# Loading the key cache as four heads of 32 partitions: a change to a two-block cached-attention kernel

## The chip, the cores and the metric

The kernel runs on one core of a Trainium2 chip. The metric is the device time of one execution in microseconds (us). The kernel before has a median of 908.98 us over 3 runs (905.89 to 911.09).

A core has five instruction streams that run side by side and meet at semaphores: TensorE (PE, with its weight loads shown apart as PEld), VectorE (DVE), ScalarE (ACT), GpSimd (POOL) and SyncE (SP). Sixteen DMA engines move data between HBM and SBUF. In this kernel SP issues all loads and ACT issues the sixteen stores.

## The reference, cut to what matters

Two independent blocks, A and B, of the same shape, each with its own inputs:

```python
B, Sq, D = 16, 64, 640;  H, Sk, Dh = 32, 512, 128        # bf16
q = (x @ wq).reshape(B, Sq, H, Dh).transpose(0, 2, 1, 3)
scores = einsum("bhqd,bhkd->bhqk", q, k_cache) * Dh ** -0.5
p = softmax(scores, axis=-1)
o = einsum("bhqk,bhkd->bhqd", p, v_cache)
block = o.transpose(0, 2, 1, 3).reshape(B, Sq, H * Dh) @ wo
out = concatenate([block_A, block_B], axis=-1)            # 16 x 64 x 1280
```

The key and the value cache are 67 MB each per block, 268 MB in all. The sum over keys in the softmax and in p·v doesn't depend on the order of the keys, as long as p and v have the same one.

## The kernel before, in words

**Tiling.** Two batches make a pair, so that 2 x 64 queries fill 128 partitions. A *step* is one head for a pair. Two steps are a *macro* (index m), two macros (four heads) a *chunk* (index c); 16 heads for one pair are a *group* (four chunks); the eight pairs of one block and one half of its heads are a *pass*. There are 4 passes, 128 chunks, 256 macros, 512 steps. The output of a pair is added up in PSUM over the 16 heads of a group; the first half's result is kept in `outp`, the second half adds it and stores.

**Work of a step or chunk.** Each kind of work has a two- to four-letter name in the code:

- QP4 (PE, line 481): the queries of four heads, 20 matmuls; QE4 (ACT, 490) copies them out.
- KX (PE, 465): transposes one K buffer, 32 instructions of 64 columns; KE (DVE, 473) copies the result into one of three `ktp` slots.
- SM (PE, 497): scores of one step, two matmuls of 512 columns that run together, one per batch; MX (DVE, 506) takes the row maximum, EX (ACT, 512) the exponential with its row sum, RC2 (DVE, 518) the reciprocals, NM (POOL, 526) multiplies and permutes the keys into the order that V has.
- TR (PE, 535) transposes p, TE (ACT or DVE, 544 and 546) copies it out, PV4 (PE, 556) multiplies by V for a chunk, OE4 (ACT, 564) copies out.
- OP (PE, 572): output product, columns 0 to 511, for one macro. At the end of a group OX (PE, 582) does columns 512 to 639 for all 16 heads at once, and OVP/OXP (ACT, 590 and 595; first half) or OVF/OXF (DVE, 600 and 605; second half) take the result out, then ST stores.

**What sets the order.** Templates written out by hand (`PE_T`, `ACT_T`, `DVE_T`, `POOL_T` in `Cfg`, lines 31 to 39) give each kind an offset in macros or chunks and a nominal time in a chunk's period; `build_plan` repeats them for all chunks and sorts. Every engine runs its list in order. `build_plan` derives the dependences from named resources (buffers and PSUM banks) and turns them into semaphore waits. In the list of PE a chunk runs SM four times, KX, PV4, OP, TR, KX, TR, OP, then OX in the last chunk of a group, then QP4.

PSUM has eight banks: one for OP, one shared by QP4 and PV4 (`QOB`), four for scores (`SB` 0 to 3; TR uses 0 and 1, OX uses 2) and two for KX.

**Loads.** LDK (line 651) brings for macro m and one batch two heads, 64 partitions each, 8 keys (2 KB) per partition: 256 KB. Two of them make one of ten K buffers, and KX of macro m needs both. LDV (660) brings two heads for one batch: 256 KB, 1 KB runs; four make one of five V buffers. LDWQ (629) and LDWO (637) bring the weights of four heads in two parts each, into six slots.

SP issues the loads in one list. `pace_loads` (line 338) adds a wait to most of them: it steps through a planned timeline of PE and of the transfers (constants `PE_NS`, `RATE`, `QUEUE_NS`, `START_NS`) and ties each load to the PE operation after which it's to be issued, so that about `QUEUE_NS` of work is ahead of it. A load therefore starts when PE reaches a certain place in its own program.

Of the kernel before, what the change touches and what calls it, by code (L numbers as in the profile page):

```python
# [5 lines left out]
BF16 = mybir.dt.bfloat16  # L6
# [8 lines left out]
class Cfg:  # L15
    G = 4
    HH = 16
    NKU = 10
    NVB = 5
# [6 lines left out]
    NT = 4  # L26
# [4 lines left out]
    PE_T = (("SM", 0, 0, 0.0), ("SM", 0, 1, 0.21), ("SM", 1, 0, 0.43), ("SM", 1, 1, 0.64), ("KX", 2, 0, 0.96),  # L31
            ("PV4", -2, 0, 1.53), ("OP", -5, 0, 2.47), ("TR", -2, 0, 2.9), ("KX", 3, 0, 3.45), ("TR", -1, 0, 4.03),
            ("OP", -4, 0, 4.47), ("OX", -5, 0, 4.9), ("QP4", 2, 0, 4.92))
    ACT_T = (("EX", 0, 0, 1.13), ("EX", 0, 1, 1.79), ("OVP", -5, 0, 2.92), ("OE4", -2, 0, 2.95), ("EX", 1, 0, 3.52), ("EX", 1, 1, 4.18),
             ("TE", -1, 0, 4.84), ("OXP", -5, 0, 5.9), ("ST", -5, 0, 6.0), ("QE4", 2, 0, 6.27))
    DVE_T = (("MX", 0, 0, 0.44), ("MX", 0, 1, 1.06), ("KE", 2, 0, 1.68), ("RC2", 0, 0, 2.83), ("OVF", -5, 0, 2.92),
             ("MX", 1, 0, 2.97), ("MX", 1, 1, 3.59), ("TE", -2, 0, 4.21), ("KE", 3, 0, 4.83),
             ("OXF", -5, 0, 5.9), ("RC2", 1, 0, 5.98))
# [4 lines left out]
    QUEUE_NS = 800.0  # L43
    START_NS = 1030.0
    RATE = dict(LDK=384.0, LDV=344.0, LDWQ=344.0, LDWO=354.0, LDX=160.0)
    DMA_NS = dict(LDK=700.0, LDV=760.0, LDWQ=950.0, LDWO=950.0, LDX=700.0)
# [22 lines left out]
def build_plan(dims, cfg):  # L69
# [30 lines left out]
    def make_chunk(eng, kind, c, ts):  # L100
        ps_, bp, _, h0 = step_info(G * c)
        if kind == "QP4":
            return mk(eng, "QP4", c, [("xT", bp)] + [("wq", wslot(ps_, h0 // G), i) for i in range(2)], [("QOB",)], ts)
        if kind == "QE4":
            return mk(eng, "QE4", c, [], [("QOB",)] + [("qT", m % cfg.NQ) for m in (2 * c, 2 * c + 1)], ts)
        if kind == "PV4":
            return mk(eng, "PV4", c, [("pT", m % cfg.NT) for m in (2 * c, 2 * c + 1)] + [("v", c % cfg.NVB, i) for i in range(4)],
                      [("QOB",)], ts)
        return mk(eng, "OE4", c, [], [("QOB",)] + [("oT", m % cfg.NO) for m in (2 * c, 2 * c + 1)], ts)

    def make_macro(eng, kind, m, sub, ts):
# [4 lines left out]
        if kind == "KX":  # L116
            return mk(eng, "KX", m, [("kn", m % cfg.NKU, 0), ("kn", m % cfg.NKU, 1), ("ident",)], [("KTB",)], ts)
        if kind == "KE":
            return mk(eng, "KE", m, [], [("KTB",), ("ktp", m % cfg.NKT)], ts)
        if kind == "SM":  # L120
            return mk(eng, "SM", (m, sub), [("qT", m % cfg.NQ), ("ktp", m % cfg.NKT)], [("SB", g % cfg.NS)], ts)
# [13 lines left out]
        if kind == "OP":  # L135
            return mk(eng, "OP", m, [("oT", m % cfg.NO), ("wo", wslot(ps_, h0 // G), m % 2)], [("OUTB",)], ts)
        if h0 + 2 != SPB:
            return None
        if kind == "OX":
            return mk(eng, "OX", m, [("oT", i % cfg.NO) for i in range(m + 1 - MPG, m + 1)]  # L140
                      + [("wo", wslot(ps_, i), n) for i in range(HG) for n in range(2)], [("SB", 2)], ts)
# [35 lines left out]
    for ps_ in range(NPASS):  # L177
        for j in range(HG):
# [7 lines left out]
            for part in range(2):  # L186
                add(rq, at["QP4", c0, 0], at["QP4", c0, 0], 0, "LDWQ", (ps_, j, part),
                    [("wq", wslot(ps_, j), part)], (ps_, j, part), cfg.DMA_NS["LDWQ"])
                first = at["OP", 2 * c0 + part, 0]
                add(ro, first, first, 3, "LDWO", (ps_, j, part), [("wo", wslot(ps_, j), part)], (ps_, j, part),  # L190
                    cfg.DMA_NS["LDWO"])

# [7 lines left out]
    for c in range(NCHUNK):  # L200
        for j in range(2):
# [3 lines left out]
            for b in range(2):  # L205
                add(ready, first, first, 2, "LDK", (m, b), [("kn", m % cfg.NKU, b)], (m, b), cfg.DMA_NS["LDK"])
            ready = at["PV4", c - cfg.NVB, 0] if c >= cfg.NVB else NEG
            first = at["PV4", c, 0]
            for i in (2 * j, 2 * j + 1):
                add(ready, first, first, 2.5, "LDV", (c, i), [("v", c % cfg.NVB, i)], (c, i), cfg.DMA_NS["LDV"])  # L210
# [15 lines left out]
    def sem_key(op):  # L226
# [4 lines left out]
        if op.kind in ("LDWQ", "LDWO"):  # L231
            return ("d_" + op.kind[2:].lower(),) + op.writes[0][1:]
# [139 lines left out]
def schedule(progs, cfg):  # L372
    def nbytes(op):
        if op.kind == "LDX":
            return (op.aux[2] - op.aux[1]) * (5 << 15)
        return dict(LDK=1 << 18, LDV=1 << 18, LDWQ=5 << 16, LDWO=5 << 16)[op.kind]
# [6 lines left out]
def mha_kernel(nc, blocks, out, cfg=None):  # L383
# [32 lines left out]
    with contextlib.ExitStack() as es:  # L416
# [9 lines left out]
        kn_ring = sb("kn_ring", [128, NKU, 2, 8, DH], BF16)  # L426
# [327 lines left out]
```

## Time and profile before

| What | Value |
|---|---|
| Median of 3 runs | 908.98 us |
| Profiled execution: its own time | 908.61 us |
| Profiled execution: span, first to last instruction | 906.8 us |
| TensorE clock granted, mean | 0.992 |
| PE busy / DVE / ACT / POOL | 836.8 / 722.4 / 652.5 / 416.8 us |
| Loads issued by SP | 1,094 |
| Moved | 297.51 MB, mean 328 GB/s |
| Median from issue to landing, K and V loads | 5.3 to 5.4 us |

How to read it: busy times are unions of instruction intervals, so engines overlap. "Idle before" a group is the time its engine waited just ahead of it, with what ended the wait; "issue" there means that the profile shows nothing that it waited for. A wait counts for the total only if the engine is the one that sets the pace at that place. The trace also has every instruction's start and every DMA packet with its size and duration; counts over these records are named as such.

### The profile page before, as it was taken

The numbers are of one execution on the slowest core, as the hardware profiler recorded it, in microseconds if no ns is written. First come the engines' busy times: TensorE is split into PE (matmuls) and PEld (weight loads), VectorE is DVE, ScalarE is ACT, GpSimd is POOL, SyncE is SP. The second block draws the span as 40 slices with busy tenths as digits, with TensorE's granted clock in tenths as the row PEclk, the third lists the DMA queues.
The fourth block names the chain that finished last, engine by engine and source line by source line (L and its number), as shares of the span: only waits on it lengthen the run. The fifth ranks groups of instructions, "written<-read, shape, count | busy, mean of one in ns | idle before, by whom it ended". The sixth has DMA issues, their size and how long they took to land.

```text
span 906.8 us, 43761 instructions
## 1 busy us (share of the span) xinstructions
PE 836.8 (92%) x18944; PEld 643.6 (71%) x18944; DVE 722.4 (80%) x1184; ACT 652.5 (72%) x1441; POOL 416.8 (46%) x518
## 2 busy tenths in 40 slices
PE   5769989998999999999999899999999999999997
PEld 4547767776777777777677676777776777777775
DVE  3666878876888888888788787878887888888885
ACT  2556877876777777777777777777777767777775
POOL 1334445553444555455455444445445445444453
PEclk9998999999999999999999999999999999999999
DMA  8999999999999999999999999999999999999990
GB/s 240 306 293 317 360 296 347 360 345 295 342 335 352 341 359 364 343 351 357 293 342 352 332 360 299 342 333 357 360 329 363 336 324 360 339 351 348 353 331 17
DMA packets 245373, 297.51 MB, mean 328 GB/s; under 512 B 28096, under 2 KB 179648, under 8 KB 245184
## 3 DMA queue, kind: packets, MB, share of 16 engines
q1 hardware_dynamic: 242880, 292.10, 97.0%
q8 instruction: 151, 2.47, 1.1%
q10 hardware_dynamic: 2304, 2.62, 0.9%
q14 instruction: 38, 0.31, 0.1%
HBM read 289.41 MB, written 2.62 MB: 322 GB/s over the span
## 4 chain that ended last, share of the span: by engine, by line
PE 80%; DMA 12%; issue 3%; DVE 3%; ACT 1%; SPq 1%; DVEq 0%; ACTq 0%
PE ps L481 14%; PE ps L465 14%; PE ps L556 14%; PE ps L497 12%; PE ps L535 12%; PE ps L572 11%; DMA v_ring<-in_A_v_cache_dram 5%; PE ps L582 3%; DMA kn_ring<-in_B_k_cache_dram 3%; DMA v_ring<-in_B_v_cache_dram 2%; DVE negmax L506 1%; DMA wq_sb<-in_A_wq_dram 1%; ACT p_ring L512 1%; DMA kn_ring<-in_A_k_cache_dram 1%; DVE out_sb L600 1%
## 5 line engine op out<-in xcount | busy, mean ns | idle before, releaser
L526 POOL TENSOR_SCALAR pn_ring<-p_ring,recip 128x512 bf16<-128x512 bf16 x512 | 416.1, 842 | 480.2 <-PE ps L535 337.9
L512 ACT ACTIVATE p_ring<-ps,negmax 128x512 bf16<-128x512 f32 x512 | 347.4, 684 | 118.6 <-DVE negmax L506 113.9
L506 DVE TENSOR_REDUCE negmax<-ps 128x1 f32<-128x512 f32 x512 | 327.6, 682 | 127.6 <-PE ps L497 127.5
L473 DVE COPY ktp_ring<-ps 128x2048 bf16<-128x2048 bf16 x256 | 312.5, 1221 | 24.3 <-PE ps L465 24.0
L465 PEld LDWEIGHTS ps<-ident,kn_ring 64*128 64x128 bf16 x8192 | 136.2, 95 | 85.9 <-issue 67.9
L465 PE MATMUL ps<-ident,kn_ring 64*128 64x64 bf16 x8192 | 168.0, 191 | 17.7 <-issue 9.5
L481 PEld LDWEIGHTS ps<-xT_sb,wq_sb 128*128 128x128 bf16 x2560 | 155.1, 99 | 37.5 <-DMA wq_sb<-in_A_wq_dram 9.9
L481 PE MATMUL ps<-xT_sb,wq_sb 128*128 128x128 bf16 x2560 | 168.1, 221 | 13.6 <-DMA wq_sb<-in_A_wq_dram 10.2
L556 PE MATMUL ps<-pT_ring,v_ring 128*128 128x64 bf16 x4096 | 144.0, 194 | 23.0 <-DMA v_ring<-in_A_v_cache_dram 12.0
L535 PE MATMUL ps<-ident,pn_ring 128*128 128x128 bf16 x2048 | 158.6, 220 | 5.0 <-issue 3.6
L572 PE MATMUL ps<-wo_sb,oT_ring 128*128 128x512 bf16 x512 | 153.8, 382 | 3.0 <-issue 1.5
L535 PEld LDWEIGHTS ps<-ident,pn_ring 128*128 128x128 bf16 x2048 | 126.2, 98 | 42.6 <-issue 6.2
L556 PEld LDWEIGHTS ps<-pT_ring,v_ring 128*128 128x128 bf16 x4096 | 128.7, 98 | 32.2 <-issue 26.2
L544 ACT ACTIVATE pT_ring<-ps 128x1024 bf16<-128x1024 bf16 x128 | 131.1, 1024 | 12.4 <-PE ps L535 11.8
L497 PE MATMUL ps<-ktp_ring,qT_ring 128*64 128x512 bf16 x1024 | 135.7, 385 | 0.5 <-ACT pT_ring L544 0.2
L490 ACT ACTIVATE qT_ring<-ps 128x512 bf16<-128x512 f32 x128 | 76.5, 597 | 73.1 <-PE ps L481 73.1
L512 ACT ACTIVATION_READ_ACCUMULATOR p_ring<-ps,negmax 128x1 f32 x512 | 101.3, 198 | 0.0
L546 DVE COPY pT_ring<-ps 128x1024 bf16<-128x1024 bf16 x128 | 87.4, 683 | 17.1 <-PE ps L535 17.0
L564 ACT ACTIVATE oT_ring<-ps 128x512 bf16<-128x512 f32 x128 | 76.3, 596 | 26.7 <-PE ps L556 24.9
L497 PEld LDWEIGHTS ps<-ktp_ring,qT_ring 128*64 128x64 bf16 x1024 | 47.0, 109 | 41.1 <-issue 1.9
L582 PEld LDWEIGHTS ps<-wo_sb,oT_ring 128*128 128x128 bf16 x512 | 29.4, 98 | 16.7 <-ACT p_ring L512 13.9
L518 DVE RECIPROCAL recip<-rowsum 128x2 f32<-128x2 f32 x256 | 39.9, 156 | 1.7 <-ACT p_ring L512 1.5
(13 smaller groups left out, 102.8 us busy)
## 6 DMA issues: line engine op xcount, KB each, us to landing
kn_ring<-in_A_k_cache_dram SPq DMA_DIRECT2D x256, 256.0 KB, 5.3
v_ring<-in_A_v_cache_dram SPq DMA_DIRECT2D x256, 256.0 KB, 5.4
kn_ring<-in_B_k_cache_dram SPq DMA_DIRECT2D x256, 256.0 KB, 5.4
v_ring<-in_B_v_cache_dram SPq DMA_DIRECT2D x256, 256.0 KB, 5.4
wo_sb<-in_A_wo_dram SPq DMA_DIRECT2D x16, 320.0 KB, 5.3
wo_sb<-in_B_wo_dram SPq DMA_DIRECT2D x16, 320.0 KB, 5.9
wq_sb<-in_A_wq_dram SPq DMA_DIRECT2D x8, 384.0 KB, 5.4
wq_sb<-in_B_wq_dram SPq DMA_DIRECT2D x8, 384.0 KB, 5.7
```

The lines of the kernel that those rows point to most:

```text
L465: ins = e.transpose(kt_ps[r][:, 64 * (8 * j + t):64 * (8 * j + t) + 64], kn_ring[half, op.idx % NKU, j, t, :], ident[half, half], tile_pos ...
L473: ins = e.tensor_copy(ktp_ring[:, op.idx % NKT].rearrange("d r j s -> d r (j s)"), kt_ps_both)
L481: ins = e.matmul(qo_ps[:, i * 128:(i + 1) * 128], wq_sb[:, wslot(ps_, hh // G), kt, i * DH:(i + 1) * DH], xT_sb[:, kt, bp * 128:(bp + 1) * ...
L497: ins = e.matmul(s_bank(2 * m + sub)[64 * j:64 * j + 64, :], qT_ring[:, m % NQ, sub, 64 * j:64 * j + 64], ktp_ring[:, m % NKT, sub, j, :], ...
L506: ins = e.reduce_max(negmax[:, r:r + 1], s_bank(g), axis=AX.X, negate=True)
L512: ins = e.activation(p_ring[:, g % NP, :], s_bank(g), ACTF.Exp, bias=negmax[:, r:r + 1], scale=1.0, accum_out=rowsum[:, r:r + 1])
L526: ins = e.tensor_scalar(dst, src, recip[:, r:r + 1], 1.0, ALU.mult, ALU.mult)
L535: ins = e.transpose(pt_bank(m)[:, 128 * i:128 * i + 128], pn_ring[:, (2 * m + sub) % NPN, t * 128:(t + 1) * 128], ident[:, :])
L544: ins = e.activation(dst, pt_bank(op.idx), ACTF.Copy)
L546: ins = e.tensor_copy(dst, pt_bank(op.idx))
L556: ins = e.matmul(qo_ps[:, col:col + 64], v_ring[:, c % NVB, j, i, t, :], pT_ring[:, (2 * c + i // 2) % NT, i % 2, t, 64 * j:64 * j + 64], ...
L572: ins = e.matmul(out_ps, oT_ring[:, m % NO, sub, :], wo_sb[:, wslot(ps_, hh // G), hh % G, 0:N0], start=(hh == 0), stop=(hh == SPB - 1))
```

## The change

- A K buffer now holds one batch and four heads of a chunk, 32 partitions per head and 16 keys (4 KB) per partition, loaded by one DMA of 512 KB. Before it held two batches and two heads, in two DMAs. As a macro's scores need both batches, SM now reads both `ktp` slots of its chunk, and KX and KE run one macro further ahead (offsets 3 and 4 in place of 2 and 3).
- SM reads its keys as 16 runs of 32 columns with a step of 64 columns, where it read 512 in a row. NM writes with a step of four elements where it was two.
- V comes in loads of 512 KB (two per buffer, 1 KB runs as before), weights in one load per slot of 640 KB. SP issues 550 loads.
- Nine K buffers in place of ten, six V buffers in place of five, two `pT` buffers in place of four.
- In the list of PE, QP4 comes ahead of the second OP and OX. ACT runs QE4 ahead of OXP; DVE runs OVF after TE, OXF after the last RC2.
- The constants of `pace_loads` change: `QUEUE_NS` 600 for 800, K rate 405 for 384, transfer times for the larger loads.

```diff
-    NKU = 10
-    NVB = 5
+    NKU = 9
+    NVB = 6
...
-    NT = 4
+    NT = 2
...
-    PE_T = (("SM", 0, 0, 0.0), ("SM", 0, 1, 0.21), ("SM", 1, 0, 0.43), ("SM", 1, 1, 0.64), ("KX", 2, 0, 0.96),
-            ("PV4", -2, 0, 1.53), ("OP", -5, 0, 2.47), ("TR", -2, 0, 2.9), ("KX", 3, 0, 3.45), ("TR", -1, 0, 4.03),
-            ("OP", -4, 0, 4.47), ("OX", -5, 0, 4.9), ("QP4", 2, 0, 4.92))
+    PE_T = (("SM", 0, 0, 0.0), ("SM", 0, 1, 0.21), ("SM", 1, 0, 0.43), ("SM", 1, 1, 0.64), ("KX", 3, 0, 0.96),
+            ("PV4", -2, 0, 1.53), ("OP", -5, 0, 2.47), ("TR", -2, 0, 2.9), ("KX", 4, 0, 3.45), ("TR", -1, 0, 4.03),
+            ("QP4", 2, 0, 4.47), ("OP", -4, 0, 5.59), ("OX", -5, 0, 6.02))
     ACT_T = (("EX", 0, 0, 1.13), ("EX", 0, 1, 1.79), ("OVP", -5, 0, 2.92), ("OE4", -2, 0, 2.95), ("EX", 1, 0, 3.52), ("EX", 1, 1, 4.18),
-             ("TE", -1, 0, 4.84), ("OXP", -5, 0, 5.9), ("ST", -5, 0, 6.0), ("QE4", 2, 0, 6.27))
-    DVE_T = (("MX", 0, 0, 0.44), ("MX", 0, 1, 1.06), ("KE", 2, 0, 1.68), ("RC2", 0, 0, 2.83), ("OVF", -5, 0, 2.92),
-             ("MX", 1, 0, 2.97), ("MX", 1, 1, 3.59), ("TE", -2, 0, 4.21), ("KE", 3, 0, 4.83),
-             ("OXF", -5, 0, 5.9), ("RC2", 1, 0, 5.98))
+             ("TE", -1, 0, 4.84), ("QE4", 2, 0, 6.0), ("OXP", -5, 0, 6.5), ("ST", -5, 0, 6.55))
+    DVE_T = (("MX", 0, 0, 0.44), ("MX", 0, 1, 1.06), ("KE", 3, 0, 1.68), ("RC2", 0, 0, 2.83),
+             ("MX", 1, 0, 2.97), ("MX", 1, 1, 3.59), ("TE", -2, 0, 4.21), ("OVF", -5, 0, 4.75), ("KE", 4, 0, 4.83),
+             ("RC2", 1, 0, 5.98), ("OXF", -5, 0, 6.5))
     POOL_T = (("NM", 0, 0, 3.0), ("NM", 0, 1, 3.85), ("NM", 1, 0, 6.1), ("NM", 1, 1, 6.95))
...
-    QUEUE_NS = 800.0
+    QUEUE_NS = 600.0
...
-    RATE = dict(LDK=384.0, LDV=344.0, LDWQ=344.0, LDWO=354.0, LDX=160.0)
-    DMA_NS = dict(LDK=700.0, LDV=760.0, LDWQ=950.0, LDWO=950.0, LDX=700.0)
+    RATE = dict(LDK=405.0, LDV=344.0, LDWQ=344.0, LDWO=354.0, LDX=160.0)
+    DMA_NS = dict(LDK=1300.0, LDV=1500.0, LDWQ=1950.0, LDWO=2150.0, LDX=700.0)
...
-            return mk(eng, "SM", (m, sub), [("qT", m % cfg.NQ), ("ktp", m % cfg.NKT)], [("SB", g % cfg.NS)], ts)
+            return mk(eng, "SM", (m, sub), [("qT", m % cfg.NQ)] + [("ktp", (m - m % 2 + j) % cfg.NKT) for j in range(2)], [("SB", g % cfg.NS)], ts)
...
-                               ktp_ring[:, m % NKT, sub, j, :], start=True, stop=True, tile_position=(0, 64 * j))
+                               ktp_ring[:, (m - m % 2 + j) % NKT, m % 2, :, sub, :], start=True, stop=True, tile_position=(0, 64 * j))
...
-            src = p_ring[:, g % NP, :].rearrange("q (th tl pp) -> q th tl pp", th=2, tl=4)
-            dst = pn_ring[:, g % NPN, :].rearrange("q (tl pp th) -> q th tl pp", tl=4, th=2)
+            src = p_ring[:, g % NP, :].rearrange("q (a tl pp) -> q a tl pp", a=4, tl=4)
+            dst = pn_ring[:, g % NPN, :].rearrange("q (tl pp a) -> q a tl pp", tl=4, a=4)
...
-            src = blocks[blk][1][2 * bp + j, h0:h0 + 2].rearrange("hs (p t) d -> (hs p) (t d)", t=8)
-            ins = e.dma_start(kn_ring[:, m % NKU, j].rearrange("p t d -> p (t d)"), src)
+            src = blocks[blk][1][2 * bp + j, h0:h0 + G].rearrange("h (p t) d -> (h p) (t d)", t=16)
+            ins = e.dma_start(kn_ring[:, op.idx % NKU].rearrange("p t d -> p (t d)"), src)
...
-            h0 = (ps_ % NHALF) * HH + hh0 + n
-            src = blocks[blk][2][2 * bp + j, h0:h0 + 2].rearrange("g (p t) d -> p g (t d)", p=128)
-            ins = e.dma_start(v_ring[:, c % NVB, j, n:n + 2].rearrange("p g t d -> p g (t d)"), src)
+            h0 = (ps_ % NHALF) * HH + hh0
+            src = blocks[blk][2][2 * bp + j, h0:h0 + G].rearrange("g (p t) d -> p g t d", p=128)
+            ins = e.dma_start(v_ring[:, c % NVB, j], src)
```

## The prediction

> **What bounds the kernel now.** I read the page first, then PE's waits between 70 and 890 us, then timelines of single chunks, then the packets.
>
> ```profile
> PE 836.8 (92%) x18944; PEld 643.6 (71%) x18944; DVE 722.4 (80%) x1184; ACT 652.5 (72%) x1441; POOL 416.8 (46%) x518
> ...
> GB/s 240 306 293 317 360 296 347 360 345 295 342 335 352 341 359 364 343 351 357 293 342 352 332 360 299 342 333 357 360 329 363 336 324 360 339 351 348 353 331 17
> ...
> q1 hardware_dynamic: 242880, 292.10, 97.0%
> q8 instruction: 151, 2.47, 1.1%
> ```
>
> Two resources are nearly full: PE is busy for 92% of the span, the load queue q1 for 97% of the engines' time. Note q8: 151 loads of 16 KB that bring the engines' own instructions.
>
> ```profile
> 647.20 1.05 PE L497 MATMUL ps<-ktp_ring,qT_ring 128*64 128x512 bf16 x8
> ...
> 652.14 1.28 PE L481 MATMUL ps<-xT_sb,wq_sb 128*128 128x128 bf16 x20
> 653.35 0.84 PE L497 MATMUL ps<-ktp_ring,qT_ring 128*64 128x512 bf16 x6
> ```
>
> A chunk that waits for nothing takes 653.35 - 647.20 = 6.15 us from scores to scores; counted over the instruction records, at least half of the 96 ordinary chunks take just that, and an undisturbed one with OX takes 7.06. So PE needs 96 x 6.15 + 31 x 7.06 = 809.3 us; the records give 875.1, from the first scores at 15.4 us to those of the last chunk at 890.6. Of these 65.8 us of waiting, 17.3 fall in the first seven intervals, to 77 us. PE's waits behind that:
>
> ```profile
> PE ps L465 <- issue: 9.5, 10, 2.8
> PE ps L556 <- DMA v_ring<-in_B_v_cache_dram: 5.0, 6, 1.6
> PE ps L535 <- issue: 3.6, 4, 1.8
> PE ps L582 <- ACT p_ring L512: 3.5, 11, 0.3
> PE ps L481 <- issue: 3.3, 7, 1.2
> PE ps L556 <- issue: 2.8, 3, 2.0
> PE ps L556 <- DMA v_ring<-in_A_v_cache_dram: 2.3, 5, 1.3
> PE ps L465 <- DMA kn_ring<-in_B_k_cache_dram: 2.1, 5, 1.2
> ...
> PE ps L465 <- DMA kn_ring<-in_A_k_cache_dram: 0.5, 1, 0.5
> ```
>
> Late data (the four DMA rows) cost 9.9 us, OX waiting for an exponential 3.5. The largest kind is "issue". What it is shows in one stop:
>
> ```profile
> 213.01 0.49 PE L465 MATMUL ps<-ident,kn_ring 64*128 64x64 bf16 x22
> 216.30 0.32 PE L465 MATMUL ps<-ident,kn_ring 64*128 64x64 bf16 x10 [2.80 <-issue]
> ```
>
> PE stops in the middle of one KX, where no wait is written. In the packet records 49 such stops after 70 us (32 us by start times) end 1.2 to 1.8 us after a 16 KB instruction packet, and nearly all stand at the same place of a count of 256 PE instructions. PE has run out of instructions. How late that packet starts goes with what q1 has issued and not yet landed: 2.1 us after a fixed place of the stream at 1.3 to 1.6 MB, 2.9 at 1.9 to 2.2 MB, 3.3 above. By the margins of the single blocks, all of them 0.2 us later would make the stops 10 us longer in all, 0.35 us later 19; 0.35 us earlier, 14 shorter, 0.5 earlier, 18. So a full load queue slows PE twice, through late data and late instructions.
>
> **The change, part by part.** The sum is made against the profiled execution: 908.6 us (span 906.8 and 1.8 around it), 0.4 below the median of 908.98.
>
> *Packets of K.* Median packet times are 46 ns at 1 KB and 84 at 2 KB: 38 per KB, so I estimate 160 at 4 KB. K takes 65,536 x 84 / 16 = 344 us of each engine now, then 32,768 x 160 / 16 = 328: 16 less. 544 loads fewer save 16 semaphore packets of 9.3 ns each: 5 us. Together 21 us of engine time, 2.4% of some 885 for which the engines are loaded. None of it is on PE's path as such. It counts through the queue: less is in flight when an instruction block is asked for. Bounds: nothing gained to 0.5 us earlier (-18), with the larger loads pulling the other way (a rival below). I take -9.
>
> *Larger loads and one macro more of lead.* Following each load's wait to the PE operation that opens it, and the PE time from there to its use: for K the median lead grows from 10.8 to 15.8 us, for V from 9.9 to 16.3; at the pass boundary, where weights come in, the smallest K lead grows from 3.2 to 8.7. Landing takes 5.4 now; a load of 512 KB takes about 0.7 longer (K loads land 0.68 apart). 8.7 covers 6.1, 3.2 does not cover 5.4. So of 9.9 us of late data I take 8 away; bounds 0 and -9.9.
>
> *Start.* The first scores now need three K buffers ahead of the second wq load: 512 KB more, 2 x 0.68 = +1.4 us. Leads are about 3 to 5 us there in both kernels, so the waits of the first seven intervals stay. Bounds 0 and +5 (seven chunks, each 0.7 later as a whole load lands at once).
>
> *QP4 ahead of OP and OX.* OX's wait of 3.5 us for the exponential is covered by QP4's 1.1 us. What comes instead, at a group's end:
>
> ```profile
> 671.48 0.59 PE L572 MATMUL ps<-wo_sb,oT_ring 128*128 128x512 bf16 x2
> 671.92 1.07 PE L582 MATMUL ps<-wo_sb,oT_ring 128*128 128x128 bf16 x16
> 672.41 1.04 ACT L544 ACTIVATE pT_ring<-ps 128x1024 bf16<-128x1024 bf16 x1
> 673.31 0.30 ACT L595 ACTIVATE outp<-ps 128x128 f32<-128x128 f32 x1
> 674.03 0.84 PE L497 MATMUL ps<-ktp_ring,qT_ring 128*64 128x512 bf16 x6
> ```
>
> OX now ends right ahead of the next scores, and the third pair of these writes OX's bank. With the same durations ACT has TE to 673.45, QE4 (0.60) to 674.05, OXP (0.30) to 674.35; the third pair is due at 674.03 + 2 x 0.21 = 674.46. It just fits; if it is 0.3 late, all of PE stands behind it, and in 32 groups that is 10 us. In the second-half passes OXF (0.29) has the same room on DVE, with the next row maxima behind it; OVF now stands behind TE, ends just ahead of QP4's end, and the second OP waits for it. I take +1.5, so -2 together; bounds -3.5 and +6.
>
> *Scores from 16 runs of 32 columns.* No row has a moving operand with gaps. Below nothing is excluded, as the 512 columns stay. Above: QP4's matmuls start 55.8 ns apart for 128 columns, SM's pair takes 213 for 512, 53.3 per 128; if each of 15 breaks cost that 2.5 ns, 512 pairs would lose 19 us. I take 0: the nearest row's loss is one per instruction, and the instruction stays one.
>
> *NM with a step of four.* POOL takes 842 ns per step and idles for more than half the span. RC2 comes every 3 us, so two NM may take 1.5 us each before anyone waits: hidden up to 1.5, 0 taken, a gain excluded by the same 512 elements.
>
> *The rest.* SM's second `ktp` slot is filled a macro earlier (KE runs from 1.7 to 2.9 us of the period before), `pT` is read by PV4 1.7 us before the next TE: 0. KX, KE, TR, PV4 keep shapes and counts. The nine and six buffers hold as many bytes. SP has half the issues, each past fewer others. The new order of PE changes no mode switch: 0.
>
> Sum: 908.6 - 9 - 8 + 1.4 - 2 = 891.0.
>
> A check from the other side: loads are under way until some 885 us; 21 less is 864, and with the last 22 us behind them 886, below the sum, so the transfers would not forbid 891.
>
> **Rivals.** (1) *K comes no faster*: HBM and not the packet is the limit. Then the -9 falls away, and two of the eight of late data stay: 908.6 - 6 + 1.4 - 2 = 902. For it: no slice passes 364 GB/s. Against: the 2 KB packets' median is 16 x 2048 / 84 = 390 GB/s. The Trainium skill, "DMA: Bandwidth & Descriptors", section "Where 436 GB/s comes from", says that for HBM to SBUF the HBM side binds, at about 358 GB/s a core; by that rule this rival holds, and the packets' 390 speak against it.
>
> (2) *Slower: instruction blocks wait longer behind loads of 512 KB.* Longer leads let the transfers fall further behind before PE waits, so more bytes are ahead of a block. If blocks start 0.7 us later (one more 256 KB ahead), the stops grow by 45 us by the margins above: 908.6 + 45 - 8 + 1.4 - 2 = 945; at 0.2 us later the gain shrinks to 910. It decides from there. For it: the correlation with the bytes in flight. Against: blocks behind 2 KB packets stopped PE no more often (20% of blocks) than behind 1 KB ones (26%), and there are 2.4% fewer engine-microseconds. The Trainium skill, same page, section "Queues, rings and completion order", says that an engine serves its queues in turn, packet by packet; by that rule a block would not wait behind q1's depth at all, which the growth from 2.1 to 3.3 us contradicts.
>
> (3) *The gapped operand costs* its 19 us: 910.
>
> (4) *The queue empties far enough* that the stops lose 25 of 32 us: 875.
>
> **How the numbers follow.** Forecast 0.58, (1) 0.13, (2) 0.13, (3) 0.07, (4) 0.09. No change means within 0.5%, about 4.5 us of 909, about what a measurement of this kernel can tell: 904.4 to 913.5. Forecast and (4) are faster, (1) mostly (0.09 of 0.13): 0.76. Same: 0.04 of (1), 0.04 of (3), 0.03 of (2): 0.11. Slower: the rest of (2) and (3), 0.13. The range runs from 876, which leaves most of (4) out, to 911, which takes in (1) and (3) and leaves most of (2) out; the forecast's own is 880 to 902.
>
> **What would show it.** Right: a packet of 4 KB near 160 ns; the DMA rows of PE's waits after 70 us below 2 us; L582's wait for ACT gone; SM's pairs still 0.21 apart; NM below 1.5 us; "issue" rows together smaller than 22 us. Wrong: "issue" above 30 us; a new PE wait at SM for L595's or L605's successor; first scores after 20 us.

## The result, and the profile after

The changed kernel is slower: median 916.46 us (910.79 to 925.84, 11 runs) against 906.16 us (899.49 to 911.09, 11 runs) for the kernel before on the same chip. The ratio is 1.0108, 95% interval 1.0071 to 1.0145. The forecast was 891, on the other side. (Disturbed runs are left out of every ratio, so a ratio isn't the quotient of the medians beside it: for e6 below that would be 1.0037, its ratio is 1.0063; where an experiment's profiled run was such a one, its profile isn't used.) The profiled execution of after took 913.25 us, span 911.5. That is 4.7 us of span above the profiled execution of before, while the medians are 10.3 apart: the two profiles show less than half of the loss.

From the page of after: busy times of the engines, two DMA queues, the group of NM, and two rows of the DMA issues (count, KB each, median us from issue to landing).

```profile
PE 821.3 (90%) x18693; PEld 634.0 (70%) x18944; DVE 722.9 (79%) x1184; ACT 646.3 (71%) x1441; POOL 666.2 (73%) x518
...
q1 hardware_dynamic: 201408, 292.06, 94.0%
q8 instruction: 150, 2.46, 1.1%
...
L520 POOL TENSOR_SCALAR pn_ring<-p_ring,recip 128x512 bf16<-128x512 bf16 x512 | 665.5, 1420 | 235.1 <-PE ps L529 205.7
...
kn_ring<-in_A_k_cache_dram SPq DMA_DIRECT2D x128, 512.0 KB, 5.9
v_ring<-in_A_v_cache_dram SPq DMA_DIRECT2D x128, 512.0 KB, 6.0
```

q1 carries the same bytes in 41,472 fewer packets and is loaded for 94.0% of the engines' time, where it was 97.0%: 880 us became 857. Landing takes half a microsecond longer. POOL's NM went from 842 to 1,420 ns, and POOL from 417 to 666 us. (PE's 18,693 matmuls are not a change of work: some records of OP are missing from this trace; what is counted below goes by weight loads, 18,944 in both.)

PE's waits of after between 70 and 890 us (us in total, times, longest). The lines have moved: KX is now 460, QP4 475, SM 491, TR 529, PV4 550, OP 566, OX 576.

```profile
PE ps L460 <- issue: 15.1, 23, 1.9
PE ps L475 <- issue: 13.0, 16, 2.1
PE ps L550 <- issue: 5.3, 8, 1.5
PE ps L566 <- issue: 3.3, 2, 2.4
PE ps L491 <- issue: 2.4, 3, 1.3
PE ps L566 <- POOL pn_ring L520: 1.7, 2, 0.9
PE ps L529 <- issue: 1.1, 3, 0.6
PE ps L529 <- ACT p_ring L506: 0.6, 1, 0.6
PE ps L550 <- DMA v_ring<-in_A_v_cache_dram: 0.5, 1, 0.5
```

Two things are gone, as planned: late data (9.9 us in the four DMA rows of before, 0.5 here) and OX's wait for the exponential (3.5). The "issue" rows have grown from 22 to 40 us, most of all in KX (9.5 to 15.1) and QP4 (3.3 to 13.0). One such stop in the timeline of after:

```profile
660.31 1.05 PE L491 MATMUL ps<-ktp_ring,qT_ring 128*64 128x512 bf16 x8
661.30 0.38 PE L460 MATMUL ps<-ident,kn_ring 64*128 64x64 bf16 x13
662.48 0.46 PE L460 MATMUL ps<-ident,kn_ring 64*128 64x64 bf16 x19 [0.81 <-issue]
```

It is the stop of the prediction: in the middle of KX, where no wait is written, after a 16 KB instruction packet. I count, in all profiles alike, the places where a block of 256 PE instructions ends (after the first 12 blocks), and call it a stop where PE is over 0.2 us late there and an instruction packet landed 0.9 to 1.8 us earlier. Before has 31 us of these stops, after 52. The packet starts 2.65 us (mean) after a fixed place of PE's stream in before, 3.01 in after.

An undisturbed chunk still takes 6.15 us. The 4.7 us between the two spans are made up of -2.3 to the start of the eighth chunk, +5.5 from there to the last (813.9 and 819.4 us), and +1.6 behind it. In the middle part the stops give +21, late data -9.4, OX's wait -3.5: +8 together; the other -2.6 is not accounted for. The wait rows alone give nearly the same: "issue" +18.2, DMA -9.4, all others -2.1, together +6.7. One of these others is new: two waits of OP for NM (1.7 us).

### The profile page after: what moved, and what is told of

Read it like the earlier page. It is cut to its first block, busy times and chain, and to the rows that moved or that the text cites. A ratio compares the mean times of both kernels' runs of the same rounds, so it can differ in the third digit from the quotient of the medians.

```text
span 911.5 us, 42783 instructions
## 1 busy us (share of the span) xinstructions
PE 821.3 (90%) x18693; PEld 634.0 (70%) x18944; DVE 722.9 (79%) x1184; ACT 646.3 (71%) x1441; POOL 666.2 (73%) x518
## 4 chain that ended last, share of the span: by engine, by line
PE 85%; issue 6%; DMA 5%; DVE 1%; POOL 1%; ACT 1%; SPq 0%; ACTq 0%
PE ps L460 16%; PE ps L475 15%; PE ps L550 14%; PE ps L529 13%; PE ps L491 13%; PE ps L566 10%; PE ps L576 3%; DMA v_ring<-in_A_v_cache_dram 3%; DMA wq_sb<-in_A_wq_dram 1%; POOL pn_ring L520 1%; DVE negmax L500 1%; DMA kn_ring<-in_A_k_cache_dram 1%; DVE ktp_ring L467 1%; ACT p_ring L506 0%; SPq L636 0%
## 5 line engine op out<-in xcount | busy, mean ns | idle before, releaser
L520 POOL TENSOR_SCALAR pn_ring<-p_ring,recip 128x512 bf16<-128x512 bf16 x512 | 665.5, 1420 | 235.1 <-PE ps L529 205.7
L460 PE MATMUL ps<-ident,kn_ring 64*128 64x64 bf16 x8192 | 170.3, 191 | 26.0 <-issue 15.1
L475 PEld LDWEIGHTS ps<-xT_sb,wq_sb 128*128 128x128 bf16 x2560 | 150.4, 99 | 19.1 <-issue 15.3
L566 PE MATMUL ps<-wo_sb,oT_ring 128*128 128x512 bf16 x261 | 98.2, 380 | 21.8 <-issue 3.5
L491 PEld LDWEIGHTS ps<-ktp_ring,qT_ring 128*64 128x64 bf16 x1024 | 44.7, 109 | 76.4 <-issue 44.2
L566 PEld LDWEIGHTS ps<-wo_sb,oT_ring 128*128 128x128 bf16 x512 | 36.0, 98 | 9.1 <-issue 4.5
```

The lines of the kernel that those rows point to most:

```text
L460: ins = e.transpose(kt_ps[r][:, 64 * t:64 * t + 64], kn_ring[half, op.idx % NKU, t, :], ident[half, half], tile_position=(64 * r, 0))
L475: ins = e.matmul(qo_ps[:, i * 128:(i + 1) * 128], wq_sb[:, wslot(ps_, hh // G), kt, i * DH:(i + 1) * DH], xT_sb[:, kt, bp * 128:(bp + 1) * ...
L491: ins = e.matmul(s_bank(2 * m + sub)[64 * j:64 * j + 64, :], qT_ring[:, m % NQ, sub, 64 * j:64 * j + 64], ktp_ring[:, (m - m % 2 + j) % NK ...
L520: ins = e.tensor_scalar(dst, src, recip[:, r:r + 1], 1.0, ALU.mult, ALU.mult)
L566: ins = e.matmul(out_ps, oT_ring[:, m % NO, sub, :], wo_sb[:, wslot(ps_, hh // G), hh % G, 0:N0], start=(hh == 0), stop=(hh == SPB - 1))
```

## The experiments

The expectations are quoted as they were written before each run. The first word behind each label says which kernel was edited. First a table: the ratio to before with its interval, the stops, the mean time from the fixed place of PE's stream to the start of the instruction packet, and the granted TensorE clock, a mean over the executions behind the ratio, for the kernel and for the before beside it. (e2, e11 and e12 are given in the text; stops and packet waits are of one execution each.)

| Kernel | Ratio to before | Stops, us | Packet wait, us | Clock, kernel / before |
|---|---|---|---|---|
| before | 1 | 31 | 2.65 | - |
| after | 1.0108 (1.0071 to 1.0145) | 52 | 3.01 | 0.991 / - |
| e1: after, planned later | 1.0262 (1.0195 to 1.0329) | 51 | 2.95 | 0.984 / 0.993 |
| e3: after, 256 KB loads, 2 KB packets | 1.0165 (1.0092 to 1.0237) | 43 | 2.78 | 0.987 / 0.993 |
| e4: after, NM with the old step | 1.0193 (1.0118 to 1.0268) | 53 | 2.98 | 0.988 / 0.993 |
| e5: after, half of V | 0.9730 (0.9638 to 0.9822) | 11 | 2.01 | 0.992 / 0.992 |
| e6: before, new order | 1.0063 (1.0021 to 1.0105) | 33 | 2.66 | 0.988 / 0.992 |
| e7: before, buffers of after | 1.0003 (0.9963 to 1.0044) | - | - | 0.991 / 0.992 |
| e8: before, V and weights in large loads | 1.0101 (1.0048 to 1.0155) | 36 | 2.66 | 0.992 / 0.992 |
| e9: after, old order | 1.0039 (1.0006 to 1.0072) | 35 | 2.84 | 0.993 / 0.991 |
| e10: e3, old order | 1.0034 (0.9998 to 1.0070) | 36 | 2.75 | 0.992 / 0.991 |
| e13: before, OX alone behind QP4 | 1.0094 (1.0057 to 1.0130) | 41 | 2.69 | 0.988 / 0.992 |
| e14: after, OP alone back | 1.0084 (1.0044 to 1.0124) | 51 | 2.94 | 0.992 / 0.992 |
| e15: before, first loads earlier | 0.9938 (0.9903 to 0.9974) | - | - | 0.993 / 0.992 |
| e16: e9, first loads earlier | 0.9953 (0.9914 to 0.9993) | 41 | 2.83 | 0.995 / 0.991 |
| e17: after, first loads earlier | 1.0029 (0.9997 to 1.0061) | 48 | 2.95 | 0.994 / 0.991 |

The clock is a rival that none of these runs tests. Over 205 of the executions behind the ratios, taken kernel by kernel, 0.001 less of granted clock goes with 0.5 us more. A difference of 0.004, as in e13 and e16, is then worth some 2 us, or 0.2%, an estimate from these executions. It is no correction, since a kernel that waits more may have the lower clock for that reason: e2, the slowest, has 0.91. But what differs by 0.3% or less is not settled by these ratios.

### Is the queue too deep because the loads are planned too early? (e1)

```diff
-    QUEUE_NS = 600.0
+    QUEUE_NS = -800.0
```

> The changed kernel, each load issued 1.4 us later in the planned queue (QUEUE_NS -800 for 600); nothing else. Theory, queue depth: PE's stops for instruction blocks (60 of 137 blocks, 51.6 us, against 38 and 30.9 before) grew because more of the loads' bytes are ahead of a block when it is asked for. 1.4 us at 350 GB/s are 0.5 MB less in flight; by the slope before (1.1 us per 0.8 MB) blocks start 0.6 to 0.7 us earlier and the stops shrink to 15 to 20 us, while late data come back to at most 8 us: 885 to 895 us, below the kernel before (906). Rival, packet size: an engine finishes 4 KB packets before it turns to a block, whatever the depth: stops stay at 45 to 55 us and the time at 914 to 922.

924.07 us against 901.31. The expectation failed: after the start nothing moved. The time lies outside both ranges (885 to 895, 914 to 922); the stops are those of the rival. Loads in flight when a block is asked for (a load counts whole until it has landed) had a median of 2.1 MB in both, the stops stayed at 51 us, and the stretch from the eighth to the last chunk took 819.0 us where after took 819.4. Only the start changed: the eighth chunk began at 86.1 us, in after at 73.5 (starts of the eighth chunk are counted, here and below, from the first load, 0.8 us into the span). So the planned constant doesn't set the steady queue. That transfers lag behind the plan and the queue is then as deep as the buffers allow would explain it, but isn't shown. That the start answers to it comes back below.

### The size of the loads (e2, e3)

e2 splits each 512 KB K load into two of 64 partitions, e3 into two of 8 keys on all 128; both also split V and the weights as before. The K edit of each:

```diff
 e2
+            src = blocks[blk][1][2 * bp + j, h0:h0 + 2].rearrange("h (p t) d -> (h p) (t d)", t=16)
+            ins = e.dma_start(kn_ring[64 * b:64 * b + 64, m % NKU].rearrange("p t d -> p (t d)"), src)
 e3
+            src = blocks[blk][1][2 * bp + j, h0:h0 + G].rearrange("h (p t) d -> (h p) t d", t=16)[:, 8 * b:8 * b + 8, :]
+            ins = e.dma_start(kn_ring[:, m % NKU, 8 * b:8 * b + 8, :], src)
```

> The changed kernel with the loads cut as before (K in two of 64 partitions, still 4 KB packets; V in four of 256 KB; weights in two parts), all else as changed. Theory, queue depth by load size: bytes in flight fall from a median of 2.1 MB to about 1.85, blocks start 0.35 us earlier, stops shrink from 52 to about 31 us, time 893 to 900. Rival, packet size: stops stay near 50 us, time 912 to 920.

1,247.84 us, ratio 1.3797 (1.3686 to 1.3909), outside both ranges. That says nothing of the size of loads; it shows that loads of 4 KB packets on 64 partitions are bad ones here: 297.5 MB in 1,248 us are 238 GB/s. So the question went to e3, with the packets of 2 KB.

> As the one with small loads, but K in two loads of 128 partitions and 8 keys each, so 2 KB packets at the same layout. Theory, queue depth by load size: as with 4 KB packets apart from 16 us of engine time more, 895 to 906, stops 30 to 40 us. Rival, packet size: the stops fall to about 31 us only here, not with 4 KB packets: 893 to 900.

916.05 us, and the stops are still 43 us, again above both ranges. Neither the 512 KB loads nor the 4 KB packets are needed for the loss. That the stops are 9 us fewer than in after may come from either; with the old order, below, the same step takes nothing away.

### The slower NM (e4)

```diff
-            src = p_ring[:, g % NP, :].rearrange("q (a tl pp) -> q a tl pp", a=4, tl=4)
-            dst = pn_ring[:, g % NPN, :].rearrange("q (tl pp a) -> q a tl pp", tl=4, a=4)
+            src = p_ring[:, g % NP, :].rearrange("q (th tl pp) -> q th tl pp", th=2, tl=4)
+            dst = pn_ring[:, g % NPN, :].rearrange("q (tl pp th) -> q th tl pp", tl=4, th=2)
```

> The changed kernel with NM writing at a step of two elements as before; this leaves p in the wrong order of keys for V, the work is the same otherwise. NM should fall from 1420 to about 842 ns. Theory, queue depth: NM is hidden at both durations (1.5 us are free for each), so 913 to 920 and stops of 45 to 55 us as in the changed kernel. Rival, GpSimd: the longer NM holds up TR and PE through short waits booked elsewhere: below 908.

NM's group in the page of e4:

```profile
L520 POOL TENSOR_SCALAR pn_ring<-p_ring,recip 128x512 bf16<-128x512 bf16 x512 | 416.7, 844 | 489.0 <-PE ps L529 351.3
```

NM fell from 1,420 to 844 ns, POOL from 666 to 417 us, and nothing came of it: 917.67 us where after has 916.46, and from the eighth chunk to the last 819.6 where after takes 819.4. (The ratio of e4 is the higher one because before ran at 901.31 on the chip that e1 to e4 shared; the intervals overlap.) The 250 us on POOL were hidden, to within the 0.8% or so that these ratios can tell.

### Do the stops follow the load of the queue? (e5)

From the seventh chunk on each V load brings two heads of four; PV4 still runs, on old data for the others.

```diff
+            n = G if c < NVB else G // 2
-            src = blocks[blk][2][2 * bp + j, h0:h0 + G].rearrange("g (p t) d -> p g t d", p=128)
-            ins = e.dma_start(v_ring[:, c % NVB, j], src)
+            src = blocks[blk][2][2 * bp + j, h0:h0 + n].rearrange("g (p t) d -> p g t d", p=128)
+            ins = e.dma_start(v_ring[:, c % NVB, j, 0:n], src)
```

> The changed kernel with only two of four heads of V loaded from the seventh chunk on (half of V's bytes, 64 MB, left out; the old data in the buffers are used). Theory, the load queue makes PE stop for instructions: with a queue that empties the stops fall from 52 us to below 10 and the time to 855 to 870 us, the span that PE needs by its undisturbed chunks with start and end. Rival, the stops belong to PE and its program: they stay at 40 to 55 us, and the time above 900.

878.68 us: 27 less than the 905.91 of before on the same chip, 38 less than after (on another chip), though PE has the same instructions. The stops were expected below 10 us and the time at 855 to 870; both came out just above. From its page:

```profile
q1 hardware_dynamic: 138944, 228.10, 81.8%
```

and its waits of PE in the same window:

```profile
PE ps L475 <- issue: 7.3, 8, 2.0
...
PE ps L566 <- issue: 0.7, 3, 0.2
...
PE ps L460 <- issue: 0.2, 1, 0.2
```

KX's "issue" row fell from 15.1 to 0.2, the stops from 52 to 11 us, the packet wait from 3.01 to 2.01 us. With q1 at 82% in place of 94% instructions mostly come in time; QP4's row, 7.3 of 13.0, is what is left. This is the causal test: nothing but loads on q1, with their bytes and packets, was taken away.

### The parts of the change alone (e6, e7, e8)

e6 is before with the new order on PE, ACT and DVE, and its old loads:

```diff
-            ("OP", -4, 0, 4.47), ("OX", -5, 0, 4.9), ("QP4", 2, 0, 4.92))
+            ("QP4", 2, 0, 4.47), ("OP", -4, 0, 5.59), ("OX", -5, 0, 6.02))
```

> The kernel before with QP4 ahead of the second OP and OX alone, with the matching places of QE4, OVF, OXF and OXP. By the prediction's step: 2 to 5 us less (OX's 3.5 us of waiting go, little comes), ratio 0.994 to 0.998. Rival, the transfers pace the kernel, so a wait that goes comes back as another: ratio 0.998 to 1.003. Rival, the order itself costs: above 1.005.

909.22 us against 905.91: the order that I priced at -2 costs 0.6%. PE's waits of e6:

```profile
PE ps L481 <- issue: 14.8, 16, 4.0
PE ps L556 <- DMA v_ring<-in_A_v_cache_dram: 5.7, 5, 1.9
PE ps L465 <- issue: 5.3, 9, 1.9
```

OX's wait is gone, and QP4's "issue" row (L481) went from 3.3 to 14.8. 16 of the 18 blocks that end inside QP4 stop there, 8 of 19 did in before. But KX's row fell from 9.5 to 5.3, and all stops together only went from 31 to 33 us: they don't account for the 0.6%. In this profile the middle part takes 818.7 us, 4.8 more than in before, and in it the clock is granted at half for 17 us where it was for 3.4; at half speed that is up to 6.8 us. So this one profile can't show the cost of the order, and by the estimate above some 1.7 of the 5.7 us in the ratio go with the clock.

e7 takes the buffers alone, e8 the large loads of V and the weights alone (K as in before; the edit of V is shown, that of the weights is like it):

```diff
 e7
-    NKU = 10
-    NVB = 5
+    NKU = 9
+    NVB = 6
...
-    NT = 4
+    NT = 2
 e8
-            for i in (2 * j, 2 * j + 1):
-                add(ready, first, first, 2.5, "LDV", (c, i), [("v", c % cfg.NVB, i)], (c, i), cfg.DMA_NS["LDV"])
+            add(ready, first, first, 2.5, "LDV", (c, j), [("v", c % cfg.NVB, j)], (c, j), cfg.DMA_NS["LDV"])
...
```

> The kernel before with nine K buffers, six V buffers and two pT buffers alone. Queue depth theory: the leads hardly change, ratio 0.997 to 1.004. Rival, the sixth V buffer lets loads run further ahead and the queue deepen: stops 10 us longer, ratio 1.008 to 1.015.

> The kernel before with V in loads of 512 KB and weights in 640 KB alone (K as before, 256 KB and 2 KB packets). Queue depth by load size: bytes in flight rise from 1.8 to about 2.0 MB, blocks start 0.2 to 0.3 us later, stops 31 to about 41 to 46 us: ratio 1.008 to 1.018, that is, most of the loss. Rival, the size of K's packets: ratio 0.998 to 1.004.

The buffers are free (904.79 us, 1.0003). Large V and weight loads cost before 1.0% (912.06 us). The ratio is inside the expected range, the reason given for it is not confirmed: stops of 41 to 46 us were expected and 36 came, blocks were to start 0.2 to 0.3 us later and the packet wait stayed at 2.66 us. Late V data did not grow either (7.0 us in its two rows, 7.3 in before), and the middle part takes 813.7 us where before takes 813.9. The leads are short there (the median V load lies ready 4.9 us before its use and takes 6.1 to land; in before 4.7 and 5.4), but that this is why e8 loses was not shown.

### After without the new order (e9, e10)

e9 is after with the reverse of e6's edit, the longer lead of KX and KE kept; e10 is the same on e3 (256 KB loads, 2 KB packets).

```diff
-            ("QP4", 2, 0, 4.47), ("OP", -4, 0, 5.59), ("OX", -5, 0, 6.02))
+            ("OP", -4, 0, 4.47), ("OX", -5, 0, 4.9), ("QP4", 2, 0, 4.92))
```

> The changed kernel with PE, ACT and DVE in the order of before (OP and OX ahead of QP4, OVF, OXF, OXP, QE4 at their old places; KX and KE still one macro further ahead). The kernel before with the new order alone was 0.6% slower. If the order costs here as there: 0.4 to 0.8% under the changed kernel (1.011 over before), so ratio 1.003 to 1.007, and the stops at QP4's line back to 3 to 6 us from 13. Rival, the order is worth what I predicted (OX's wait): 1.012 to 1.016.

> The changed kernel with loads cut as before and K in 2 KB packets (two loads of 128 partitions and 8 keys) and the old order as well; what is left of the change is K's layout, the lead, the buffers and the planner's constants. If load size (1.0% in the kernel before) and order (0.6%) make the whole loss: ratio 0.995 to 1.004. Rival, K's layout or the lead costs too: above 1.006.

910.74 and 909.57 us against 904.73. So of the 1.1% the order is 0.7, all the rest 0.4, each known to some 0.4 (the intervals of e9 and after just touch); packets of 4 KB and loads of 512 KB against 2 KB and 256 KB make no difference that can be measured (1.0039 and 1.0034). The waits of e9:

```profile
PE ps L460 <- issue: 10.6, 16, 1.8
PE ps L475 <- issue: 5.6, 8, 1.2
PE ps L550 <- issue: 4.8, 8, 1.4
PE ps L576 <- ACT p_ring L506: 4.1, 12, 0.9
PE ps L550 <- DMA v_ring<-in_A_v_cache_dram: 2.7, 2, 2.2
```

OX's wait for ACT is back (4.1), and 17 us of stops have gone with it. Late data is 2.7 where before had 9.9, so the lead works; but the stops are 35 us, not the 22 that the forecast needed (31 less 9). In this profile the middle part takes 808.2 us, 5.7 less than in before, but its eighth chunk begins 3.5 us later.

### The transfers alone (e11, e12)

The loads of each kernel in their order and with their buffers' sizes, no compute; zeros are stored.

```diff
-            run_program(sync, progs["sp"])
...
+            for op in progs["sp"]:
+                if op.count > 1:
+                    sync.wait_ge(sems[op.sem], 16 * (op.count - 1))
+                ins = emitters[op.kind](sync, op)[1]
+                ins.then_inc(sems[op.sem], 16)
...
```

> Only the loads of the kernel before, in its order, each waiting for the last load into the same buffer and for nothing else; all computation left out, zeros stored. By median packet times they take 817 us, by the mean ones 885. Theory, the transfers' own capacity paces the kernel: above 865 us. Rival, the load queue hurts by its depth and not by its capacity: 800 to 840.

> Only the loads of the changed kernel, as above. By the prediction's estimate 21 us less than those of before (16 from 4 KB packets, 5 from fewer loads). Rival, HBM sets the rate and not the packets: within 5 us of those of before.

822.96 and 800.92 us. The transfers of after are 22.0 us shorter, where I had estimated 21. The last line of the DMA part, first of e11, then of e12:

```profile
HBM read 289.41 MB, written 2.62 MB: 355 GB/s over the span
```

```profile
HBM read 289.41 MB, written 2.62 MB: 366 GB/s over the span
```

So HBM is no cap at 355, and the packets do what was said of them. The kernels need 906 and 916 us: the transfers alone are not the limit, and a relief of 22 us on them bought nothing in the kernel.

### What in the order costs (e13, e14)

The first idea was that QP4 must not come ahead of OP. e13 puts OX alone of PE's operations behind QP4 in before, with QE4, OXP and OXF at their places of after; e14 puts OP back ahead of QP4 in after, with OVF at its old place.

```diff
 e13
-            ("OP", -4, 0, 4.47), ("OX", -5, 0, 4.9), ("QP4", 2, 0, 4.92))
+            ("OP", -4, 0, 4.47), ("QP4", 2, 0, 4.92), ("OX", -5, 0, 6.02))
 e14
-            ("QP4", 2, 0, 4.47), ("OP", -4, 0, 5.59), ("OX", -5, 0, 6.02))
+            ("OP", -4, 0, 4.47), ("QP4", 2, 0, 4.92), ("OX", -5, 0, 6.02))
```

> The kernel before with OX alone moved behind QP4 (PE: ..., TR, OP, QP4, OX; QE4, OXP and OXF as in the changed kernel, OVF at its old place). If the order costs because PE reaches the instruction block behind QP4's start 0.43 us sooner, without an OP in front (stops at QP4 5.1 us before, 17.8 with the new order): the stops at QP4 stay at 4 to 9 us, OX's wait of 3.5 to 5 us goes, ratio 0.992 to 0.998. Rival, OX at the end of the period is what costs, through its bank and the next scores: ratio 1.003 to 1.008.

> The changed kernel with the second OP back ahead of QP4 and OX behind it, OVF at its old place. By the same theory stops at QP4 fall from 15.2 to 5 to 9 us and the time to 0.997 to 1.004 of the kernel before (the changed one with the whole old order was 1.004, less OX's wait of 5.5 us). Rival, OX at the end costs: 1.007 to 1.013.

913.71 us (1.0094) and 915.47 (1.0084): the idea fell. OP's place shows no cost, and OX behind QP4, with what moves along on ACT and DVE, is what costs: clearly in e13, less so in e14, whose interval overlaps that of e9. The rival was that OX holds the bank of the next scores. In the trace it is late there, but not on the path: the weight loads of the third pair of scores wait for OXP and OXF,

```profile
PEld ps L497 <- ACT outp L595: 4.7, 16, 0.3
PEld ps L497 <- DVE out_sb L605: 4.4, 14, 0.3
```

(waits of the weight loads of e13), which puts that pair's weights 0.2 us later than in an ordinary chunk; the KX behind it starts 0.006 us later, so PE has made it up. What is left are the stops: 41 us for 31. Over the six pairs of profiles that differ in the order (before with e6 and e13, e9 with after and e14, e10 with e3, e16 with e17) the stops rise by 2 to 17 us, 10 on average, and OX's wait of 3.5 to 4.8 us goes; the some 6 us that remain fit the ratios, which rise by 0.4 to 1.3%. In e13 the packet wait is 2.69 us, as good as the 2.65 of before, so the blocks are not later on average; that they are late where it matters more was not shown. Why OX's place does this stays open.

### The start (e15, e16, e17)

e1 had shown that the start answers to the plan. e15 issues the first 70 loads of before 1.5 us earlier in the plan; e16 and e17 the first 36 of e9 and of after 1.7 us earlier.

```diff
 e15
-        issue = start - cfg.START_NS - cfg.QUEUE_NS
+        issue = start - cfg.START_NS - cfg.QUEUE_NS - (1500.0 if len(gates) < 70 else 0.0)
 e16 and e17
-        issue = start - cfg.START_NS - cfg.QUEUE_NS
+        issue = start - cfg.START_NS - cfg.QUEUE_NS - (1700.0 if len(gates) < 36 else 0.0)
```

> The kernel before with its first 70 loads issued 1.5 us earlier in the planned queue. Issued 1.4 us later, the changed kernel's eighth chunk began at 86 us in place of 74. If the start is starved by the planned waits, the eighth chunk begins 3 to 8 us earlier than 76 us and the ratio is 0.992 to 0.997; if the transfers are full there, 0.998 to 1.003.

901.25 us against 905.32: by the ratio 0.6% faster than before. Where the time was won, no profile that can be used shows.

> The changed kernel with the old order on PE, ACT and DVE, and its first 36 loads planned 1.7 us earlier. My account of the 1.1%: from the start of the eighth chunk to that of the last, the undisturbed profiles with OX ahead of QP4 take 808.2 to 813.9 us whatever the loads, those with OX behind it 818.7 to 821.1; and the kernels with 512 KB of K per load begin the eighth chunk some 4 us later than those without (73.5 to 79.7 against 71.1 to 75.9). Theory: the start is held up by the planned waits of the loads, as it was in the kernel before: the eighth chunk begins 3 to 5 us earlier than in the old-order run without this (79.4), the later stretch stays at 808 to 814, the time falls to 904 to 908, ratio 0.992 to 1.002. Rival: at the start the transfers are the limit, or the K buffers that need a macro more of lead; then the eighth chunk begins at 78 to 80 and the ratio stays at 1.004.

> The changed kernel with its own order, and its first 36 loads planned 1.7 us earlier. If the place of OX is what the steady part pays for, the stretch from the eighth to the last chunk stays at 819 to 821 us though the start is the same as in the run with the old order beside it; both kernels begin the eighth chunk within 2 us of each other, and this one is 5 to 11 us slower, ratio 1.002 to 1.010. Rival: the difference between the orders was one of the start and of single executions; then the two stretches are within 3 us of each other and so are the times.

904.84 and 908.31 us against 908.45. The eighth chunk begins at 72.2 us in e16 (79.4 in e9) and at 70.8 in e17 (73.5 in after). So in all three kernels waits of the plan held up the start, for 0.6 to 0.9% by the ratios (for e16 and e17 against a kernel measured on another chip). Some of that goes with the clock: of the 4.3 us by which e16 beats before, 2.2 by the estimate above, and ahead of the eighth chunk the clock is at half for 6.8 us in e16's profile and for 13.7 in e9's. e15 and e16 beat both kernels of the study, and cannot be told from each other.

On the order they gave half an answer. By the ratios e17 is 0.8% above e16 (by the medians 0.4%), as after is 0.7% above e9. But my expectation that the profiles would show it in the stretch from the eighth to the last chunk failed: 816.8 us in e16, 817.3 in e17. Over the profiles of whole kernels with full loads, those with OX ahead of QP4 take 808.2 to 816.8 us there (before, e8, e9, e10, e16), those with OX behind it 817.3 to 821.1 (after, e1, e3, e4, e6, e13, e14, e17). No overlap, but the single executions of one side lie 9 us apart, so a pair of them can't size it; and with half of the time at half clock taken off, the two sides do overlap (807.8 to 813.7 and 810.2 to 819.6, e6 and e3 being the ones that move in). The direction rests on the ratios. The stops of e16 and e17 stand at 41 and 48 us.

## Why the prediction was wrong

The sum was 908.6 - 9 - 8 + 1.4 - 2 = 891.0. By its terms:

- **-9, fewer stops for instructions: wrong in sign.** This step failed first. The premise held: 4 KB packets take 159 ns (160 estimated), and the transfers alone got 22 us shorter (21 estimated). The inference "less is in flight when a block is asked for" did not: a median of 2.1 MB was in flight, 1.84 in before. Counted in bytes not yet moved, which the size of the loads doesn't round up, it is 1.19 and 1.11 MB: not less, but not much more. A faster queue was not left emptier, most likely since the longer leads let more be asked for: e10, with the loads and packets of before, has 2.1 MB too (1.24 not yet moved). Blocks came 0.36 us later, and the stops rose by 21 us. Without the new order (e9) blocks came 0.19 us later and the stops rose by 4, to 35.
- **-8, late data: right.** 9.9 became 0.5 us; 2.7 in e9. The median slack of a K load, from its landing to its use, rose from 5.1 to 10.8 us. But it came back as stops: in e9 the DMA rows lost 7.2 us and the "issue" rows gained 4.6, in e16 9.9 and 10.8. And e16 and e15, both with an early start, one with the new layout, leads and loads, the other with the old, are 0.9953 and 0.9938. The -9 and -8 together were worth nothing that these runs can tell (to some 0.5%).
- **+1.4, the start: small, and a larger thing stood beside it.** The first scores came 2.2 us later, the eighth chunk at 73.5 us where it was 75.9 (single executions of after's layout lie between 73.5 and 79.7, of before's between 71.1 and 77.8). I took the waits of the first seven intervals as given; the plan made some of them, and by the ratios 0.6 to 0.9% lay there in both kernels.
- **-2, QP4 ahead of OP and OX: wrong in sign.** OX's 3.5 us went as said, and its bank fits as worked out: 0.006 us of harm. Yet the order costs 0.6% in before and 0.7% in after (part of it may be the clock), by the place of OX and what moves with it (e13, e14). I had counted waits by semaphore alone and not asked what the order does to the places where blocks end: QP4's stops went from 5 to 18 us in e6 and stand at 15 in after. In e6 KX's stops shrank at the same time, so this names the place and not the reason, which stays open.
- **0 for NM: the cover held, the duration didn't.** I had no row for a step of four and took the 842 ns as if it stayed; it became 1,420, just below the 1.5 us that I had worked out as cover. **0 for the scores** from 16 runs was right: the pairs still start 0.24, 0.22 and 0.22 us apart, as in before, and an undisturbed chunk takes 6.15 us. **0 for the buffers** was right (e7).

Of the rivals, (1) falls: K comes faster, and e12 reads and writes 366 GB/s over its whole span (362 for the reads alone). The Trainium skill ("DMA: Bandwidth & Descriptors", section "Where 436 GB/s comes from") has the HBM side bind at about 358 GB/s a core; the measurement, on the one core that this kernel uses, is slightly above it. (3) and (4) did not come. (2) has the right side and the right mechanism, later instruction blocks: its working gave 19 us of stops for 0.35 us later, and 21 came with 0.36. Its cause was not the load of 512 KB, as it had it: e10 has nearly the same stops and time as e9 with loads of 256 KB. And it is not the whole: most of the 21 us comes with the order (e9 has 35), whose stops (e13) grow with the packets no later on average. So that 19 and 21 agree is in part luck.

The point that I weighed wrongly can be read in the profile of before: the stops and the late data are two faces of one full queue. I had seen that a full queue "slows PE twice", and then booked savings on both as if they were separate.

## What to carry to other kernels

When two waits come from the same full resource, taking one away (by a longer lead) can let the other grow; in this kernel only less traffic (e5: 22% fewer bytes on q1, 38 us) or an earlier start (0.6 to 0.9%) brought the time down. Instruction loads use the DMA engines too (q8, 150 loads): a stop in the middle of an operation with nothing written that could wait, ending just after a 16 KB instruction packet, is to be added up over the kernel before and after a change in the order of instructions, even one that removes a visible wait. And a change made of a layout, leads, loads and an order should be measured part by part: here the order alone cost some 0.7%, all the rest 0.4%, in numbers so small that the granted clock has to be read beside each ratio.

## What the runs showed of the hardware

- A tensor_scalar of 128x512 bf16 on GpSimd takes 842 to 844 ns when it writes every second element, in runs of 64, and 1,420 ns when it writes every fourth, in runs of 32; after and e4 differ in this alone.
- Within the changed kernel the stops fall with the load of the DMA queue, not in proportion: 52 us with q1 at 94.0% of the engines' time, 11 at 81.8%. The share alone doesn't set them: before has 31 us at 97.0%.
- Granted clock and time go together: over 205 executions, 0.001 of clock goes with 0.5 us of some 905.
- Loads of 4 KB packets on 64 partitions brought the kernel to 1,248 us (238 GB/s); the same bytes on 128 partitions gave 916, in packets of 2 KB as of 4 KB.
- Loads alone: 292 MB in 823 us with K in 2 KB packets (88 ns each, median), 801 us in 4 KB ones (164 ns).
